# Two units of q, k, v made as one Strassen-like group of seven products, in a planned kernel for windowed attention beside an MLP

## The chip, the cores and the metric

The kernel runs on one core of one Trainium2 chip. The metric is device microseconds of that core for one execution; the time before is the median of three executions. A profile is one further execution, recorded instruction by instruction.

## The reference, cut to what matters

The input x has 2048 positions (S) of 640 numbers (D). Everything is float32. Two branches read it, and a gate mixes them:

```python
x = A_x
g = sigmoid((x * gate_w).sum(-1, keepdims=True))
# branch A: 32 heads of 20, window of 8 keys at distance 0, 2, 4 ... 14
qkv = x @ A_wqkv                       # (2048, 640) @ (640, 1920)
logits[s, w] = q[s] . k[s - 2 * w] * 20 ** -0.5
o[s] = sum_w softmax(logits)[s, w] * v[s - 2 * w]
a = o @ A_wo                           # (2048, 640) @ (640, 640)
# branch B: Dense, Mish, Dense
h = x @ B_w1 + B_b1                    # (2048, 640) @ (640, 1728)
b = (h * tanh(softplus(h))) @ B_w2     # (2048, 1728) @ (1728, 640)
return g * a + (1 - g) * b
```

## The kernel before, in words

**Products.** TensorE (PE) multiplies blocks of 128x128 by 128 rows of up to 512 columns. To keep float32 accuracy each operand is held as a pair of tiles, a rounded part (`hi`) and what is left of it (`lo`), and one product is three matmuls: hi·hi, hi·lo, lo·hi (`mm3`, lines 462 to 464). Making a pair is called a split: ScalarE (ACT) copies the raw tile to `hi` (line 412), and VectorE (DVE) or GpSimd (POOL) subtracts to get `lo` (line 415).

**The work is cut so.** The 2048 positions are two halves P = 0 and 1, each of two blocks of 512 (`tb`). Eight units u make q, k and v: unit u is half P = u // 4 and eight heads `hq` = u % 4; its weights are 496 columns wide (480 of q, k, v and 16 of the first dense layer; 512 for hq = 0, which carries the gate too). A unit has eight slots of 128 positions; a slot is 5 blocks of D times 3 matmuls, 15 matmuls, summed in one PSUM bank of the ring `qb` and then copied out by three ACT instructions (`qkv_evac`, lines 626 to 630) to the tile `kvq`. The first dense layer (`Quad` for P = 0, `Plain` for P = 1) makes two blocks of 128 hidden values for a whole half. In a `Quad` a 2x2 product of blocks is done with seven products, as in Strassen's method: weight and x blocks are added and subtracted beforehand (`combined`, line 816; `x_forms`), some banks are seeded from others by ACT (`seed`, line 920), and DVE adds two banks at the end (`added`, line 936). The forms of x for that, `FORM[P, "t1" .. "t4", i]`, lie in SBUF. `sums_of` prepares added blocks of w2 and wo in the same way. Then come the second dense layer (`mlp2`) and the output projection (`wo_part`), for P = 0 and P = 1.

**Attention** runs on DVE, unit by unit, beside the PE's work: for each pair of slots a multiply q·k (line 519), a reduction over the 20 numbers of a head (522), a softmax of four slots (maximum 540, subtraction 541, exp on ACT 542, a copy of the weights on ACT 543, sum 548, reciprocal 549, times the gate 550, weights times that 551), multiplies with v (560) and a reduction over the window (564). The result is turned (line 475) and written to DRAM as `o`.

**What sets the order.** The kernel's text adds tasks to a planner (`Plan`); each has an engine, a cost in ns, tasks that it waits for and buffers that it takes from rings (three PSUM banks each in `qb` and `sb`, 24 pairs, 8 raw tiles, 6 tiles `hb`). `Plan.run` plays these costs through and gives each engine a fixed list of instructions; on the chip every engine follows its list and waits on semaphores. When several tasks are ready, the one with the lowest rank goes first, then the one that was added first. So the order in which the text calls `unit`, `quads`, `mlp1_last` and so on sets the order on PE, and DVE takes attention steps only where no task of lower rank is ready. Tasks for `"ANY"` go to POOL, or to DVE where they are due (`NEAR`, `PATIENCE`). Transfers are issued by SyncE (SP), line 429; the planner takes `LAG["SP"]` ns and the size for their landing.

**Lines that the prediction speaks of.** 412 and 415 (split), 462 to 464 (matmuls), 519, 522, 560, 564 (the four long attention steps), 475 (turn), 816 (sum of two tiles), 920 (seed), 926 (Mish of the first layer), 936 (sum of two banks), 626 to 630 (a slot's way out of PSUM), 1173 (sums behind the second dense layer's products).

Of the kernel before, what the change touches and what calls it, by code (L numbers as in the profile page):

```python
# [30 lines left out]
ROW = 2 * QF  # L31
# [35 lines left out]
class Plan:  # L67


    NEAR, PATIENCE = 8000, 2000  # L70
# [34 lines left out]
    def run(self):  # L105
# [34 lines left out]

        def fits(t):
            want = {}
            for b in t.take:
                want[b.ring] = want.get(b.ring, 0) + 1
                if b.ring.free < want[b.ring] or b.ring.line[b.ring.at + want[b.ring] - 1] is not b:
                    return False
            return True

        while left:
            again = not events or events[0][0] > now  # L150
            while again:
                again = False
                for e in self.LAG:
# [41 lines left out]
                    if e == "PE":  # L195
                        begun_pe = max(begun_pe, t.pos)
                    busy[e] = again = True
# [6 lines left out]
                    if e != "SP":  # L204
# [12 lines left out]
            if what == "done":  # L217
                left -= 1
                x.at = now
                for b in x.hold:  # L220
# [5 lines left out]
            for t in x.then:  # L226

                if (t.eng == x.eng and x.eng != "SP") != (what == "own"):
# [7 lines left out]
        return now  # L236


@with_exitstack
def kernel(ctx: ExitStack, tc: tile.TileContext, x, wq, wo, w1, b1, w2, out):  # L240
# [12 lines left out]
    NPAIR, NRAW, NH = 24, 8, 6  # L253
# [110 lines left out]
    w1_d = {(q, n): dram.tile([128, 2, 512], F32, name=f"wf{q}_{n}") for q in range(NQUAD + 1) for n in range(4)}  # L364
    h_d = [dram.tile([FR, 512], F32, name=f"h{tb}") for tb in range(4)]
# [133 lines left out]
    def attention(u, P, hq, ready, gates):  # L499
# [29 lines left out]
        def bounded(a, b, after):  # L529
# [4 lines left out]
            return add("ACT", 130 * (min(b, 7) - a), run, cg + after, rank=-1)  # L534

        def softmax(a, rank, after, used):
# [4 lines left out]
            t = step("DVE", 350, lambda: V.tensor_tensor(lg[:, h], lg[:, h], mx[:, h, :, None].to_broadcast([128, 4, HQ, W]), op=OP.subtract))  # L541
            e = add("ACT", 360 + 2 * TABLE, lambda: A.activation(lg[:, h], lg[:, h], AF.Exp, scale=scale), [t], rank=-1, late=1500)
            return e, add("ACT", 600, lambda: A.activation(pw_h[:, h], lg[:, h], AF.Copy), [e, used], rank=-1)

        def shares(a, rank, e, copied):
# [4 lines left out]
            step("DVE", 230, lambda: V.tensor_tensor(sm[:, h], sm[:, h], gate[:, P, h, None].to_broadcast([128, 4, HQ]), op=OP.mult), gates)  # L550
# [85 lines left out]
    def qkv(u, P, hq, between={}):  # L636
        n = columns(u)
        kv = KV[UNIT[u]]
        ev = {}
        pss = [sb_buf() if i == 3 else qb_buf() for i in range(4 if u == 0 else 0)]  # L640
        if u == 0:
# [14 lines left out]
            for kc in range(2, KC):  # L656
                for i in range(4):
# [3 lines left out]
                    if kc == KC - 1:  # L661
                        ev[i] = qkv_evac(u, P, hq, i, pss[i], last)
        for i in range(8):
            if i in ev:
                continue
            if len(pss) == i:
                pss.append(qb_buf())

            def slot(i=i):
                for kc in range(KC):  # L670
                    qkv_part(pss[i], P, u, i, kc, n)

            xs = [X[2 * P + i // 4, kc] for kc in range(KC)]
            ws = [WQ[u, kc] for kc in range(KC)]
            last = pe_add(15 * mm_ns(n), slot, sum((b.ready for b in xs + ws), []), take=[pss[i]], hold=xs + ws)
            ev[i] = qkv_evac(u, P, hq, i, pss[i], last)
            if i in between:
                between[i]()
        before = sum((freed.get((BEFORE.get(u), s), []) for s in range(8)), [])
        halo = {}  # L680
        for lo, hi, src in ((3, 7, (0, 1, 2, 3)), (0, 3, (5, 6, 7))):
            w = [ev[i][0] for i in src] + before + cg
            halo[lo] = [dma(lambda a=a, b=b, lo=lo, hi=hi: kv[a + 1:b + 1, lo:hi], lambda a=a, b=b, lo=lo, hi=hi: kv[a:b, lo + 8:hi + 8],
                            w, rank=-1.0, size=(b - a) * (hi - lo) * ROW * 4) for a, b in ((0, 112), (112, 127))]
# [1022 lines left out]
```

## Time and profile before

| | |
|---|---|
| three executions | 623.71, 624.12, 624.54 us; median 624.12 us |
| the profiled execution | 624.5 us, of which 622.7 us lie between its first and last instruction |
| busy share of that span | PE 99%, weight loads 82%, DVE 93%, ACT 56%, POOL 48% |
| matmuls | 2743 in the trace |
| bytes moved | 140.36 MB, mean 225 GB/s |
| granted TensorE clock | 1.000 |

The span is what the profile's times count in; the 1.8 us between it and the execution's own time lie before the first and after the last instruction. A matmul's time in the rows is modelled and longer than its share of the engine, since matmuls are pipelined: the distance from one start to the next is what it costs. Waits are listed by who ended them. "Busy" on PE therefore says only that there was no gap.

### The profile page before, as it was taken

The page shows a single profiled execution, that of the slowest core. Times are in us where ns is not written, and L with a number is a line of the kernel's source. Part 1 is how long each engine was busy: PE and PEld are TensorE (multiplying, and loading weights), DVE is VectorE, ACT ScalarE, POOL GpSimd, SP SyncE. Part 2 cuts the span into 40 slices and gives each one's busy share as a digit, 9 for nine tenths or more (in the row PEclk, how much of TensorE's full clock was granted, in tenths as well). Part 3 has the DMA queues.
Part 4 walks back from the last instruction along what each step waited for, and adds up shares of the span by engine and source line. Part 5 has one row for each costly group of instructions (what it writes and reads, how often), then busy time and mean ns, then how long its engine had stood idle before and what let it go on. Part 6 is the DMA issues. An engine that isn't in the chain of part 4 may idle for free.

```text
span 622.7 us, 9060 instructions
## 1 busy us (share of the span) xinstructions
PE 616.9 (99%) x2743; PEld 513.3 (82%) x2743; DVE 578.8 (93%) x554; ACT 351.3 (56%) x790; POOL 299.6 (48%) x277
## 2 busy tenths in 40 slices
PE   9999999999999999999999999999999999999997
PEld 7878888888888888888888888888888888888886
DVE  7799999999999999999999999999999999869965
ACT  6687637746675554634664545676655634546520
POOL 1487657575576557567553614787318610100000
PEclk9999999999999999999999999999999999999999
DMA  8765675595784779989976687768798755999613
GB/s 309 210 191 156 241 254 130 180 294 155 253 279 147 250 236 252 270 253 274 281 229 212 210 281 191 206 177 247 225 323 260 196 189 179 246 291 337 229 53 118
DMA packets 97600, 140.36 MB, mean 225 GB/s; under 512 B 11200, under 2 KB 51392, under 8 KB 97328
## 3 DMA queue, kind: packets, MB, share of 16 engines
q1 hardware_dynamic: 94192, 134.02, 67.3%
q0 software_dynamic: 3072, 5.51, 5.8%
q8 instruction: 21, 0.34, 0.3%
q10 hardware_dynamic: 288, 0.26, 0.1%
q14 instruction: 27, 0.22, 0.1%
HBM read 87.78 MB, written 51.00 MB: 223 GB/s over the span
## 4 chain that ended last, share of the span: by engine, by line
PE 96%; ACT 1%; DVE 1%; issue 0%; POOL 0%; DVEq 0%
PE qb L462 20%; PE qb L463 20%; PE qb L464 20%; PE sb L462 11%; PE sb L463 11%; PE sb L464 11%; PE qb L620 1%; ACT pair L412 1%; DVE raw L816 1%; PE sb L394 1%; DVE pair L415 0%; PE qb L468 0%; PE sb L469 0%; PE sb L468 0%; PE qb L469 0%
## 5 line engine op out<-in xcount | busy, mean ns | idle before, releaser
L415 POOL TENSOR_TENSOR pair<-raw,pair 128x512 fp32r<-128x512 f32 (+3 forms) x131 | 162.5, 1269 | 100.0 <-ACT pair L412 51.2
L462 PE MATMUL qb<-pair 128*128 128x512 f32 (+1 forms) x467 | 180.7, 387 | 1.0 <-ACT hb L740 1.0
L463 PE MATMUL qb<-pair 128*128 128x512 f32 (+1 forms) x467 | 180.6, 387 | 0.0
L464 PE MATMUL qb<-pair 128*128 128x512 f32 (+1 forms) x467 | 180.6, 387 | 0.0
L412 ACT ACTIVATE pair<-raw 128x512 fp32r<-128x512 f32 (+3 forms) x223 | 128.6, 610 | 56.3 <-DMA raw<-actt 18.0
L463 PE MATMUL sb<-pair 128*128 128x512 f32 (+1 forms) x294 | 113.7, 387 | 0.0
L464 PE MATMUL sb<-pair 128*128 128x512 f32 (+1 forms) x294 | 113.7, 387 | 0.0
L462 PE MATMUL sb<-pair 128*128 128x512 f32 (+1 forms) x294 | 113.7, 387 | 0.0
L462 PEld LDWEIGHTS qb<-pair 128*128 128x128 f32 x467 | 87.7, 188 | 18.5 <-ACT hb L740 1.4
L464 PEld LDWEIGHTS qb<-pair 128*128 128x128 f32 x467 | 87.6, 188 | 17.1
L463 PEld LDWEIGHTS qb<-pair 128*128 128x128 f32 x467 | 87.7, 188 | 17.0
L560 DVE TENSOR_TENSOR pr<-kvq,pg 128x1280 f32<-128x1280 f32 x64 | 93.1, 1484 | 1.0
L519 DVE TENSOR_TENSOR pr<-kvq,qg 128x2560 f32<-128x2560 f32 x32 | 90.0, 2811 | 2.3 <-ACT qg L525 1.0
L564 DVE TENSOR_REDUCE kvq<-pr 128x320 f32<-128x2560 f32 x32 | 90.2, 2818 | 0.9
L522 DVE TENSOR_REDUCE lg<-pr 128x128 f32<-128x2560 f32 x32 | 90.1, 2817 | 0.8
L626 ACT ACTIVATE kvq<-qb 128x320 f32<-128x320 f32 x63 | 27.6, 438 | 77.4 <-PE qb L464 77.3
L415 DVE TENSOR_TENSOR pair<-raw,pair 128x512 fp32r<-128x512 f32 (+2 forms) x92 | 64.7, 727 | 5.1 <-ACT pair L412 5.0
L464 PEld LDWEIGHTS sb<-pair 128*128 128x128 f32 x294 | 55.2, 188 | 11.3
L462 PEld LDWEIGHTS sb<-pair 128*128 128x128 f32 x294 | 55.2, 188 | 11.2
L463 PEld LDWEIGHTS sb<-pair 128*128 128x128 f32 x294 | 55.2, 188 | 11.2
L816 POOL TENSOR_TENSOR hb<-hb 128x512 f32<-128x512 f32 x38 | 50.2, 1337 | 23.8 <-DVE ot L475 5.8
L412 ACT ACTIVATE pair<-hb 128x512 fp32r<-128x512 f32 (+3 forms) x62 | 36.6, 590 | 8.7 <-PE qb L464 3.0
(158 smaller groups left out, 732.6 us busy)
## 6 DMA issues: line engine op xcount, KB each, us to landing
actt<-hb SPq DMA_DIRECT2D x52, 256.0 KB, 3.6
raw<-in_w SPq DMA_DIRECT2D x40, 256.0 KB, 4.5
act<-hb SPq DMA_DIRECT2D x38, 256.0 KB, 2.6
raw<-actt SPq DMA_DIRECT2D x37, 256.0 KB, 4.7
raw<-in_wq SPq DMA_DIRECT2D x30, 248.0 KB, 3.8
raw<-act SPq DMA_DIRECT2D x29, 256.0 KB, 2.9
raw<-in_x SPq DMA_DIRECT2D x23, 256.0 KB, 3.0
o<-ot SPq DMA_DIRECT2D x64, 80.0 KB, 2.7
```

The source lines that it names most:

```text
L394: nc.tensor.matmul(warm_banks[i % 3].t[:, :n], ones[:, :128], ones[:, :n], start=True, stop=True)
L412: a = add("ACT", act_ns(n), lambda: A.activation(hi(), raw(), AF.Copy), after, rank=rank, take=take, hold=hold)
L415: return (V if e == "DVE" else G).tensor_tensor(lo(), raw(), hi().bitcast(F32), op=OP.subtract)
L462: nc.tensor.matmul(ps, ah, bh, start=first, stop=False, skip_group_check=more)
L463: nc.tensor.matmul(ps, ah, bl, start=False, stop=False, skip_group_check=more)
L464: nc.tensor.matmul(ps, al, bh, start=False, stop=last, skip_group_check=more)
L519: return V.tensor_tensor(pr, window(kv, s0, 0), qg[:, :, None, :].to_broadcast([128, 2, W, QF]), op=OP.mult)
L522: V.tensor_reduce(lg_w[:, s0:s0 + 2], pr.rearrange("p s w (h d) -> p s w h d", d=DH), op=OP.add, axis=AX.X)
L560: V.tensor_tensor(pairs[:, s].rearrange("p k i (h d) -> p k i h d", d=DH), vw, pg[:, s0 + s].rearrange("p (k i) h -> p k i h", i=2)[:, :, ...
L564: V.tensor_reduce(q[:, s0:s0 + 2], pairs.rearrange("p s k i f -> p s f k i"), op=OP.add, axis=AX.XY)
L626: a = add("ACT", 330, lambda: A.activation(kv[:, 7 + s], ps.t[:, QF:3 * QF].rearrange("p (a b) -> p a b", a=2), AF.Copy), [done] + before, ...
L816: return (V if e == "DVE" else G).tensor_tensor(t.t[:, i:i + n], a.t[:, j:j + n], b.t[:, k:k + n], op=op)
```

## The change: what it does

Units 2 and 3 (heads 16 to 23 and 24 to 31 of the first half of x) are made together. They share x, so for four of the five blocks of D (0 to 3, taken as the pairs 0 with 2 and 1 with 3) the weights of the two units and the two 512-position blocks of x form 2x2 products of blocks, and these are done with seven products in place of eight, with the forms of x that the quads already have. Block 4 stays as it was (`plain`). The new class `Two` holds this, for each j of four 128-position slots:

- first stage: `a1` (s1·t1, 6 matmuls, copied by ACT to an `hb` tile and stored to DRAM), `a2` (11·x, 6 matmuls, then a DVE sum to a bank of `sb`), `a3` (s2·t2, 6 matmuls into that sum, copied by ACT and stored), `b1` and `b2` (9 matmuls each), which end two slots of unit 2;
- second stage: `c0` loads the two stored tiles, `c1` seeds a bank of `sb` from one of them by ACT, adds s3·t3 (6 matmuls), and DVE subtracts the other to a bank of `qb`; `c2` (3 matmuls) and `c3` (9 matmuls) end two slots of unit 3.

Weights are loaded as raw tiles in two goes (`wa`, `wc`), combined (eight combinations of 128x496) and split (16 pairs in place of 10). The planner counts how many transfers are in flight on SP and starts no more than eight 450-ns issues' worth; `LAG["SP"]` is 2700 for 3000, `ADDING` 4000 for 6000, `PATIENCE` 1000 for 2000; a task that sends data itself is followed when it has landed. The gate now goes into the copy of the softmax weights: four ACT instructions of 128x64 with a scale in place of one of 128x256, and DVE's multiply by the gate (line 550) is gone. The order of the steps is a list of names, `ORDER`, in place of calls with `between`; the parts of a quad (`first`, `second`, `m1` to `m4`, `l1`, `l2`) and the slots of a unit can stand there one by one. All second-half quads stay `Plain` (`KIND`), so the classes for another kind are not used.

```diff
-    NEAR, PATIENCE = 8000, 2000
+    NEAR, PATIENCE = 8000, 1000
-    LAG = {"PE": 220, "ACT": 220, "DVE": 200, "POOL": 150, "SP": 3000}
+    LAG = {"PE": 220, "ACT": 220, "DVE": 200, "POOL": 150, "SP": 2700}
-    ADDING = 6000
+    ADDING = 4000
+    FLIGHT = 8
...
+        def lanes(t):
+            return round(t.ns / 450)
...
-                    fit = [t for t in ready[e] if fits(t)]
+                    fit = [t for t in ready[e] if fits(t) and (e != "SP" or flight + lanes(t) <= self.FLIGHT)]
...
+KIND = 'PPPPPP'
+PAIRS = {2: (0, 1)}
+ORDER = """
+u.0.5 u.0.7 u.0.4 last.0 u.0.6 q.0.0.first pieces.0.1 q.0.0.m1 q.0.1.first wq.1 pieces.0.2 q.0.1.second q.0.0.second q.0.0.m3 q.0.0.m4 q.0.1.m1 last.1
...
+pieces.0.5 q.0.5.first q.0.4.l1 p.2.3.c0 q.0.5.m1 q.0.5.m4 q.0.5.second x.3.3 q.0.5.m2 x.2.1 x.3.0 p.2.0.c1 p.2.1.c1 x.3.4 p.2.0.c2 q.0.5.m3 p.2.3.c1
...
-            return e, add("ACT", 600, lambda: A.activation(pw_h[:, h], lg[:, h], AF.Copy), [e, used], rank=-1)
+            def weighted():
+                for i in range(a, a + 4):
+                    A.activation(pw_h[:, i], lg[:, i], AF.Copy, scale=gate[:, P, i:i + 1])
+
+            return e, add("ACT", 1200, weighted, [e, used] + gates, rank=-1)
...
-            step("DVE", 230, lambda: V.tensor_tensor(sm[:, h], sm[:, h], gate[:, P, h, None].to_broadcast([128, 4, HQ]), op=OP.mult), gates)
...
+        def copy(self, to, of, n, after, take=()):
+            return add("ACT", act_ns(n) + 60, lambda: A.activation(to.t[:, :n], of.t[:, :n], AF.Copy), after, rank=-0.5, take=take, hold=[to, of])
+
+        def sum_to(self, to, x, y, op, n, after, yt=None):
+            yt = yt or (lambda: y.t)
+            return add("DVE", dve_ns(n) + 80, lambda: V.tensor_tensor(to.t[:, :n], x.t[:, :n], yt()[:, :n], op=op), after, rank=SOON, kind="psum",
+                       take=[to], hold=[to, x, y])
...
+        def a1(self, j):
+            n, ep, v = self.n, qb_buf(), h_buf()
+            t = self.products(ep, j, self.fs("s1", "t1"), [], n, [ep], True)
+            self.copied[j] = c = self.copy(v, ep, n, [t], [v])
...
+            self.state["v", j] = self.store(v_d[self.u, j], v, NCOL, [c])
+
+        def a2(self, j):
+            n, al, be = self.n, qb_buf(), sb_buf()
+            t = self.products(al, j, self.xs("11", 0, 0), [], n, [al], True)
+            self.al[j], self.be[j] = al, be
+            self.seeded[j] = self.sum_to(be, al, self.v[j], OP.add, n, [t, self.copied[j]])
...
+        def b1(self, j):
+            t = self.products(self.al[j], j, self.xs("12", 0, 1) + self.plain(0, 0), [self.seeded[j]], self.n)
+            units[self.u].ready(j, self.al[j], t)
...
+        def c1(self, j):
+            ga, de, n = sb_buf(), qb_buf(), NCOL
+            (u, ut, du), (v, vt, dv) = self.state["u", j], self.state["v", j]
+            s = add("ACT", act_ns(n) + 60, lambda: A.activation(ga.t[:, :n], ut()[:, :n], AF.Copy), [du], rank=-0.5, take=[ga], hold=[ga, u])
+            t = self.products(ga, j, self.fs("s3", "t3"), [s], n)
+            self.ga[j], self.de[j] = ga, de
+            self.seeded[j] = self.sum_to(de, ga, v, OP.subtract, n, [t, dv], vt)
+
+        def c2(self, j):
+            t = self.products(self.ga[j], j, self.plain(1, 1), [self.seeded[j]], NCOL)
+            units[self.u + 1].ready(4 + j, self.ga[j], t)
+
+        def c3(self, j):
+            t = self.products(self.de[j], j, self.fs("22", "t4") + self.plain(1, 0), [self.seeded[j]], NCOL)
+            units[self.u + 1].ready(j, self.de[j], t)
```

Where the instructions stand now, at the end of the first half, just before unit 4 begins. On PE there stood the last four slots of unit 3, of 15 matmuls each, all from bank to bank of `qb` with no other engine between them; the first matmul of each, and of unit 4 behind them:

```order
L462 MATMUL qb_2026<-pair_1691,kvq2_262 128x496
...
L462 MATMUL qb_2057<-pair_1691,kvq2_262 128x496
...
L462 MATMUL qb_2086<-pair_1691,kvq2_262 128x496
...
L462 MATMUL qb_2118<-pair_1691,kvq2_262 128x496
...
L462 MATMUL qb_2143<-pair_2017,pair_1843 128x512
```

Now the last product of the quads (into sb_1972) stands there and behind it the second stage of the pair, again the first matmul of each group. `c1` of three slots j are the groups into sb_2029, sb_2034, sb_2046, each of 6 matmuls; the second group into sb_2029 is its `c2`, qb_2072 its `c3`:

```order
L494 MATMUL sb_1972<-pair_576,pair_1796 128x512
...
L494 MATMUL sb_2029<-pair_1655,pair_573 128x496
...
L494 MATMUL sb_2034<-pair_1655,pair_573 128x496
...
L494 MATMUL sb_2046<-pair_1655,pair_573 128x496
...
L494 MATMUL sb_2029<-pair_1729,pair_431 128x496
...
L494 MATMUL qb_2072<-pair_1690,pair_576 128x496
...
L494 MATMUL sb_2046<-pair_1729,pair_431 128x496
...
L494 MATMUL qb_2080<-pair_1690,pair_576 128x496
...
L494 MATMUL sb_2121<-pair_1655,pair_573 128x496
```

Groups of 15 that waited for no other engine's result became groups of 3 to 9 of which each waits for an ACT copy or a DVE sum.

On DVE, at the same place, there were attention steps (kvq0 and kvq1 are the q, k, v of two units, pr the products) and splits of weights and x for unit 4:

```order
L564 TENSOR_REDUCE kvq0_260<-pr_267 128x320
L519 TENSOR_TENSOR pr_267<-kvq0_260,qg_266 128x2560
L522 TENSOR_REDUCE lg_263<-pr_267 128x2x8x8
L560 TENSOR_TENSOR pr_267<-kvq0_260,pg_265 128x4x2x160
L415 TENSOR_TENSOR pair_2055<-raw_2007,pair_2055 128x512
L415 TENSOR_TENSOR pair_2082<-raw_2045,pair_2082 128x512
L540 TENSOR_REDUCE mx_268<-lg_263 128x32
L541 TENSOR_TENSOR lg_263<-lg_263,mx_268 128x256
```

Now the sums of the second stage (line 808, PSUM to PSUM) stand among them, the first of them behind an attention reduction (line 554, which was 522):

```order
L1144 TENSOR_TENSOR hb_2017<-hb_2009,sb_1890 128x512
L1144 TENSOR_TENSOR hb_2009<-hb_2009,sb_1932 128x512
L447 TENSOR_TENSOR pair_2020<-raw_1959,pair_2020 128x512
L572 TENSOR_REDUCE mx_276<-lg_271 128x32
L573 TENSOR_TENSOR lg_271<-lg_271,mx_276 128x256
L554 TENSOR_REDUCE lg_271<-pr_275 128x2x8x8
L808 TENSOR_TENSOR qb_2072<-sb_2029,pair_1741 128x496
L808 TENSOR_TENSOR qb_2075<-sb_2034,pair_1759 128x496
L808 TENSOR_TENSOR qb_2080<-sb_2046,pair_1861 128x496
L551 TENSOR_TENSOR pr_275<-kvq0_268,qg_274 128x2560
L554 TENSOR_REDUCE lg_271<-pr_275 128x2x8x8
L808 TENSOR_TENSOR qb_2155<-sb_2121,pair_1938 128x496
```

The bank that sb_2029 takes is free once an `added` sum (the two rows of line 1144, which was 936) has read it; the `c2` and `c3` groups on PE wait for the rows of line 808.

On ACT there were a split, the last slots' way out of PSUM and the softmax's bounds:

```order
L412 ACTIVATE pair_2082<-raw_2045 128x512
L626 ACTIVATE kvq1_261<-qb_2057 128x320
L628 ACTIVATE kvq1_261<-qb_2057 128x160
L532 ACTIVATE lg_263<-bound_76 1x8x7
L532 ACTIVATE lg_263<-bound_76 1x8x6
```

Now the seeds of the second stage (line 861) stand behind the Mish of the quads' last product (line 1132, which was 926):

```order
L444 ACTIVATE pair_2020<-raw_1959 128x512
L1132 ACTIVATE hb_2025<-sb_1972,bias_75 128x512
L861 ACTIVATE sb_2029<-pair_1741 128x496
L861 ACTIVATE sb_2034<-pair_1759 128x496
L861 ACTIVATE sb_2046<-pair_1861 128x496
L1132 ACTIVATE hb_2017<-hb_2017,bias_75 128x512
L1132 ACTIVATE hb_2009<-hb_2009,bias_75 128x512
L574 ACT_TABLE_LOAD
```

So the first `c1` on PE follows the PE group just before it only by way of two ACT instructions.

More of the change, by code (lines that the diff above doesn't have):

```diff
@@ L661, in qkv @@
                     if kc == KC - 1:
[L662 to L684, printed above, removed]
-        own = sum((list(ev[i][:2]) for i in range(8)), [])
@@ L686, in qkv, with ready @@
[L686 to L690 removed]
+                        self.ev[i] = qkv_evac(u, P, self.hq, i, pss[i], last)
+        def ready(self, i, ps, t):
+            self.ev[i] = qkv_evac(self.u, self.P, self.hq, i, ps, t)
+            quads_done.append(self.ev[i][2])
+            if len(self.ev) == 8:
+                self.ended()
@@ new lines, in slot, with run @@
+        def slot(self, i):
+            u, P, n = self.u, self.P, self.n
+            if i not in self.ev:
+                ps = qb_buf()
+                def run():
+                    for kc in range(KC):
+                        qkv_part(ps, P, u, i, kc, n)
+                xs = [X[2 * P + i // 4, kc] for kc in range(KC)]
+                ws = [WQ[u, kc] for kc in range(KC)]
+                t = pe_add(15 * mm_ns(n), run, sum((b.ready for b in xs + ws), []), take=[ps], hold=xs + ws)
+                self.ev[i] = qkv_evac(u, P, self.hq, i, ps, t)
+            if len(self.ev) == 8:
+                self.ended()
```

348 lines of the change are left out of this document (250 added, 98 removed).

## The prediction

> **What bounds the kernel now.** I read the page first: the share of each engine and the slices.
>
> ```profile
> span 622.7 us, 9060 instructions
> PE 616.9 (99%) x2743; PEld 513.3 (82%) x2743; DVE 578.8 (93%) x554; ACT 351.3 (56%) x790; POOL 299.6 (48%) x277
> ```
>
> PE has no room and DVE little. Next the waits of PE, which are two in the whole execution, together 1.8 us:
>
> ```profile
> PE qb L462 <- ACT hb L740: 1.0, 1, 1.0
> PE sb L394 <- PEq L1695: 0.8, 1, 0.8
> ```
>
> Then the stretches of 50 us. The columns are PE, weight loads, DVE, ACT, POOL, each with its count, then the granted clock, the DMA share and GB/s:
>
> ```profile
> 100.00:150.00 50.00, 50.00 (x226) 42.07 (x225) 48.00 (x38) 30.71 (x73) 31.74 (x31) 1.00 0.64 198
> 150.00:200.00 50.00, 50.00 (x226) 42.07 (x225) 47.61 (x41) 33.06 (x78) 33.13 (x28) 1.00 0.69 218
> ...
> 250.00:300.00 50.00, 50.00 (x225) 41.99 (x224) 49.00 (x36) 24.97 (x64) 30.33 (x31) 1.00 0.92 269
> ```
>
> PE is full in each and the clock stays at 1.00, so the time is matmuls times their spacing. DVE is the next engine: 48 to 49 of 50 us in the first half. A matmul taken away shortens the program only if DVE, which must then do its list in less time, doesn't make PE wait.
>
> **The matmuls removed.** For each of four j the group ends four slots (two of each unit) with 54 matmuls in place of 4 x 15 = 60, so 216 stand for 240: 24 matmuls of 496 columns go. Their price is the distance from start to start; between these two rows lie 24 starts:
>
> ```profile
> 129.94 0.38 PE L462 MATMUL qb<-pair 128*128 128x496 f32 x1
> 135.22 0.38 PE L462 MATMUL qb<-pair 128*128 128x496 f32 x1
> ```
>
> 5.28 us for 24, 0.220 each. The same count with 512 columns, used below, gives 0.2267:
>
> ```profile
> 429.64 0.39 PE L462 MATMUL sb<-pair 128*128 128x512 f32 x1
> 435.08 0.39 PE L462 MATMUL qb<-pair 128*128 128x512 f32 x1
> ```
>
> So the change takes 5.28 us from PE's work.
>
> The Trainium skill ("TensorE: Matmul & The Clock Gate", section "Wait — 56ns, not 53.3ns?") puts a streaming matmul at one column per cycle of 2.4 GHz and about 2.5 ns more. By that, an estimate, 496 columns are 209 ns and the 24 matmuls 5.0 us; the rows show 5% more per matmul, and the rows decide.
>
> **The waits added on PE.** They lie at the end of the first half, where c1, c2 and c3 stand. First the way through ACT. The seed of c1's bank stands on ACT behind the Mish of the PE group just ahead. The rows for each step: the last matmul of a slot and the start of the copy that it releases, then the Mish and a seed (mean ns of one):
>
> ```profile
> 138.96 0.38 PE L464 MATMUL qb<-pair 128*128 128x496 f32 x1
> 139.38 0.44 ACT L626 ACTIVATE kvq<-qb 128x320 f32<-128x320 f32 x1 [1.86 <-PE qb L464]
> L926 ACT ACTIVATE hb<-sb,bias 128x512 f32<-128x512 f32 x18 | 12.3, 683 | 14.4 <-PE sb L464 9.4 <-DMA actt<-hb 4.3 <-ACT hb L926 0.7
> L920 ACT ACTIVATE sb<-sb 128x512 f32<-128x512 f32 x12 | 7.1, 588 | 3.9 <-PE sb L464 3.7
> ```
>
> 0.42 from start to ACT, 0.68, 0.59, less the 0.23 that the matmul itself takes: PE waits 1.5 us at least.
>
> Second, the way through DVE. c2 and c3 wait for the first sum of line 808, row 139 of DVE's new list, behind all the attention steps that stand there before it. So I count both engines from the end of unit 0, which is where DVE's attention can start, to that sum. DVE's prices:
>
> ```profile
> L560 DVE TENSOR_TENSOR pr<-kvq,pg 128x1280 f32<-128x1280 f32 x64 | 93.1, 1484 | 1.0
> L564 DVE TENSOR_REDUCE kvq<-pr 128x320 f32<-128x2560 f32 x32 | 90.2, 2818 | 0.9
> L522 DVE TENSOR_REDUCE lg<-pr 128x128 f32<-128x2560 f32 x32 | 90.1, 2817 | 0.8
> L519 DVE TENSOR_TENSOR pr<-kvq,qg 128x2560 f32<-128x2560 f32 x32 | 90.0, 2811 | 2.3 <-ACT qg L525 1.0
> L415 DVE TENSOR_TENSOR pair<-raw,pair 128x512 fp32r<-128x512 f32 x83 | 59.6, 738 | 5.1 <-ACT pair L412 5.0
> L475 DVE STREAM_TRANSPOSE ot<-kvq 128x640 f32<-128x640 f32 x16 | 13.5, 842 | 0.3
> L936 DVE TENSOR_TENSOR hb<-hb,sb 128x512 f32<-128x512 f32 x12 | 8.1, 677 | 1.1 <-PE sb L464 0.8
> L541 DVE TENSOR_TENSOR lg<-lg,mx 128x256 f32<-128x256 f32 x16 | 7.0, 440 | 0.6
> L550 DVE TENSOR_TENSOR sm<-sm,gate 128x32 f32<-128x32 f32 x16 | 4.1, 259 | 0.4
> ```
>
> In DVE's new list, from the first q·k to the first sum of line 808 stand 11 multiplies and 11 reductions of q·k (61.9 us), 16 multiplies with v (23.7), 8 reductions over the window (22.5), 23 sums of two tiles of whatever line (at 0.68, 15.6), 6 splits (4.4), 4 turns (3.4) and 26 short softmax and gate steps (10.7, most of them like the row of line 541): 142.2 us. The means count too much, since neighbours overlap. Before, the stretch between the first row and the last one here holds 130.7 us by means and took 131.5, of which 3.0 were waits (1.1 for a transfer, the rest short ones for ACT and PE); so means give 128.5/130.7 = 0.983 of themselves, 139.8 us:
>
> ```profile
> 36.13 2.81 DVE L519 TENSOR_TENSOR pr<-kvq,qg 128x2560 f32<-128x2560 f32 x1
> ...
> 102.68 0.68 DVE L936 TENSOR_TENSOR hb<-hb,sb 128x512 f32<-128x512 f32 x1
> 103.28 2.81 DVE L522 TENSOR_REDUCE lg<-pr 128x128 f32<-128x2560 f32 x1
> ...
> 167.66 2.81 DVE L519 TENSOR_TENSOR pr<-kvq,qg 128x2560 f32<-128x2560 f32 x1
> ```
>
> PE has in the same stretch 339 matmuls of 512 columns (76.9 us) and 282 of 496 (62.0): 138.9 us. DVE starts some 1.6 us after the end of unit 0 (the copies out of PSUM and the spreading of q, by rows like the one at 139.38). So PE waits 139.8 + 1.6 − 138.9 = 2.5 us if DVE never waits, and 5.5 if its 3.0 us of waits come back. A count from the last place where DVE must wait for PE (the sum into hb_1707, 27 DVE rows ahead: 37.8 us by means, less the 0.08 that each of 18 short steps overlaps, as from 102.68 to 103.28; PE 34.6 us; 0.3 for the handing over) gives 2.0, the lower end. I take half of the DVE waits: 4.0 us. The wait of 1.0 at 42 us lies in this stretch too and is in that figure, so it comes off once: gain 5.28 + 1.0 − 4.0 = 2.3 us.
>
> **What costs nothing, with its cover.** SP gets 22 more transfers of about 0.25 MB, 5.5 MB on 140.4; they fall mostly between 70 and 170 us, where the DMA share is 0.64 to 0.69, and at 0.92 (250 to 300 us) PE didn't wait either. If that cover fails, c1's reload comes late at one transfer's wait, about the 1.1 us above. POOL's eight combinations and some splits are 10 us more on 48%. ACT gets 12 copies (7 us), and 64 weight copies of 128x64 for 16 of 128x256. No row has 128x64; the nearest are narrower and wider:
>
> ```profile
> L543 ACT ACTIVATE pw<-lg 128x256 f32<-128x256 f32 x16 | 11.4, 713 | 0.5
> L630 ACT ACTIVATE hx<-qb 128x16 f32<-128x16 f32 x63 | 11.9, 189 | 0.0
> L1025 ACT ACTIVATE raw<-raw 128x128 f32<-128x128 f32 x9 | 2.7, 314 | 0.0
> ```
>
> Four take 0.76 to 1.26 us for 0.71; I take 1.0, +4.6 us in all. DVE's sum and reciprocal hide it, and if they don't, DVE waits 0.3 us sixteen times, mostly where it has waits anyway. The multiply of line 550 frees DVE 16 × 0.259 = 4.1 us, the eight sums cost it 8 × 0.68 = 5.4. The planner's numbers move only the order.
>
> **The sum.** 624.5 of the profiled execution less 2.3 is 622.2. The median lies 0.4 under that execution: 621.8.
>
> **Rivals.** *PE waits only for the short way* (2.0 us or, if ACT alone decides, 1.5): 5.28 + 1.0 − 2.0 = 4.3 off, 619.8; 619.3 to 620.8. For it: before, DVE's list held PE up nowhere. Against: DVE's list is counted longer than PE's.
>
> *The waits fill the gain*: more of the c groups, each 3 to 9 matmuls, wait in turn, 5.1 to 7.5 us in all: 622.9 to 625.3.
>
> *DVE is late in the second half* (slower than before). The attention of units 4 to 7 moves back in DVE's list: its last reduction over the window stood at 507.7 us and is counted about 13 us later. Before, DVE waits there:
>
> ```profile
> 506.00 0.69 DVE L1173 TENSOR_TENSOR kvq<-kvq,sb 128x512 f32<-128x512 f32 x1 [0.43 <-PE sb L469]
> 507.14 0.69 DVE L1173 TENSOR_TENSOR kvq<-kvq,sb 128x512 f32<-128x512 f32 x1 [0.45 <-PE sb L469]
> 507.74 2.81 DVE L564 TENSOR_REDUCE kvq<-pr 128x320 f32<-128x2560 f32 x1
> ...
> 531.79 0.69 DVE L1173 TENSOR_TENSOR kvq<-kvq,hb 128x512 f32<-128x512 f32 x1 [3.98 <-ACT hb L1169]
> ...
> 552.70 0.69 DVE L1173 TENSOR_TENSOR kvq<-kvq,qb 128x512 f32<-128x512 f32 x1 [5.37 <-PE qb L469]
> ```
>
> 10.2 us of room, so PE was never held. Now, from the c groups to the projection's late splits, PE has 1147 and 411 matmuls (350.4 us) and DVE's 260 instructions come to 346 by means: 4.4 us of room. If DVE meets such waits again before that point, it is 10.2 − 4.4 = 5.8 late and PE waits for its splits: 621.8 + 5.8 = 627.6 (625.4 to 629). It is slower than before once those waits pass 4.4 + 2.3 + 1.2 = 7.9 us. For it: the two long waits show that DVE's list is not dense there. Against: a later attention leaves DVE work where it waited.
>
> *The clock falls.* Each wait on PE in this trace was 1.0 us or less, and the clock stayed at 1.00. At the start matmuls lie further apart:
>
> ```profile
> 0.80 3.15 PE sb L394 x10
> ...
> 5.33 0.85 PE qb L620 x2
> 6.18 0.25 PE sb L620
> 6.43 0.70 PE qb L620 x3
> ```
>
> 0.425 us each at 5.33, 0.233 each from 6.43 on: 5.4 us from 0.80 at about half pace. If a wait of 4 us in one piece brought that back, half of it, 2.7 us, would be lost: 624.5, up to 626. Against: the wait is likely in two pieces.
>
> The Trainium skill (same page, section "What's actually happening") says that an idle window of about 3.4 us makes the clock fall to half. Before has no such gap, so no row here bears it out.
>
> That the matmuls do not go is no case: PE's new list has them fewer.
>
> **How the numbers follow.** Forecast 0.42 (620.8 to 622.8), short way 0.09, waits fill the gain 0.20, DVE late 0.22, clock 0.07. A measurement here tells about 0.2%, 1.25 us, from no change: 622.9 and 625.3 are the bounds. Faster is 0.42 + 0.09 = 0.51; within is 0.20, and 0.02 of the clock's; slower 0.22 + 0.05 = 0.27. The range leaves out the upper part of the DVE case and the lowest of the short way: 619.5 to 627.6. The cases of the forecast's sign alone give 619.3 to 622.8.
>
> **What would show it.** Right: 2719 to 2721 matmuls; PE waits of 2 to 5.5 us in all between 168 and 182 us (unit 0's end near 36, then the 138.9 us of matmuls), the larger for a sum of line 808, the other for a seed of line 861; none over 1 us behind it; the clock at 1.00. Wrong: PE waits for splits after 450 us (DVE late), waits for transfers at the c groups, a clock below 1.00 there, or sums of line 808 that are done before PE comes (short way).

## The result, and the profile after

The changed kernel takes 621.9 us (median of 7 executions, 620.57 to 622.46) beside 623.88 us of the kernel before: ratio 0.9962, 95% interval 0.9951 to 0.9974. The forecast was 621.8. As the sections below show, the sum came out for a partly different reason than the prediction gave. Two executions lie far above all others of their kernel (3041.09 us of one of the kernel before, 686.61 us of one with a longer DVE, at a clock of 0.849) and are in no median or ratio.

The page of the profiled execution (622.0 us), the lines of share and count:

```profile
span 620.2 us, 9150 instructions
PE 613.0 (99%) x2719; PEld 509.3 (82%) x2719; DVE 583.5 (94%) x550; ACT 364.4 (59%) x854; POOL 312.6 (50%) x287
```

24 matmuls are gone (2743 to 2719), and DVE is busier by 4.7 us in a span shorter by 2.5. All the waits of PE:

```profile
PE sb L494 <- ACT sb L861: 1.8, 1, 1.8
PE sb L426 <- PEq L1933: 0.8, 1, 0.8
PE qb L656 <- DVE kvq L1729: 0.7, 1, 0.7
```

The wait of 1.0 us at 42 us is gone, and the seed of the first `c1` (line 861) costs 1.8 us. The wait of 0.7 at the start is new but costs nothing: the first group of three matmuls behind it begins at 6.39 us, at 6.43 in the kernel before. No wait for a sum of line 808 stands here. What does stand here is a loss that the list of waits cannot show. The stretches around the c groups, with PE's busy time and count, then the granted clock, the DMA share and GB/s:

```profile
168.00:172.00 4.00, 3.36 (x15) 1.00 0.98 325
172.00:174.00 2.00, 0.87 (x4) 1.00 0.94 306
174.00:176.00 2.00, 2.00 (x7) 0.56 1.04 375
176.00:178.00 2.00, 2.00 (x7) 0.59 1.04 382
178.00:180.00 2.00, 2.00 (x11) 1.00 1.05 364
```

PE is "busy" all through 174 to 178, but only 7 matmuls run in each 2 us, in whole or in part, beside 11 from 178 to 180: the granted clock is 0.56 and 0.59. If the clock was at half while it was down, that is (0.44 + 0.41) x 2 / 0.5 = 3.4 us at half. The same place matmul by matmul:

```profile
170.97 0.39 PE L496 MATMUL sb<-kvq,pair 128*128 128x512 f32 x1
173.13 0.49 PE L494 MATMUL sb<-pair 128*128 128x496 f32 x1 [1.77 <-ACT sb L861]
...
174.45 0.61 PE L496 MATMUL sb<-pair 128*128 128x496 f32 x1
...
176.93 0.61 PE L496 MATMUL sb<-pair 128*128 128x496 f32 x1
177.34 0.54 PE L494 MATMUL sb<-pair 128*128 128x496 f32 x1
...
177.93 0.39 PE L496 MATMUL sb<-pair 128*128 128x496 f32 x1
```

From 171.20 (the last matmul's start and its 0.23) to 173.13 PE has nothing for 1.93 us. From 174.45 to 176.93 six steps take 2.48 us, 0.413 each in place of 0.220. The nine long steps from 174.13 to 177.72 add up to 1.6 us over 0.22 each.

This does not happen in every execution. Of the 12 of the changed kernel measured here and in a later run, six had a mean clock of 1.000 and took 620.57 to 621.51 us (median 621.06), six had 0.996 or 0.997 and took 621.66 to 622.46 (median 621.97). The 621.9 is the median of seven of which four had the fall. The repeated run's profile is of an execution without it, and there PE does lose a little to a sum of line 808, too short for the list of waits: the last matmul of the third `c1` and the first of `c2` lie 0.41 us apart in place of 0.22, and the first sum on DVE has just ended:

```profile
177.47 0.39 PE L496 MATMUL sb<-pair 128*128 128x496 f32 x1
177.88 0.50 PE L494 MATMUL sb<-pair 128*128 128x496 f32 x1
```

```profile
177.16 1.83 DVE L808 TENSOR_TENSOR qb<-sb,pair 128x496 f32<-128x496 f32 x3
```

### The profile page after: what moved, and what is told of

It reads as the page before. It is cut to its first block, busy times and chain, and to the rows that moved or that the text cites. A ratio compares the mean times of both kernels' runs of the same rounds, so it can differ in the third digit from the quotient of the medians.

```text
span 620.2 us, 9150 instructions
## 1 busy us (share of the span) xinstructions
PE 613.0 (99%) x2719; PEld 509.3 (82%) x2719; DVE 583.5 (94%) x550; ACT 364.4 (59%) x854; POOL 312.6 (50%) x287
## 4 chain that ended last, share of the span: by engine, by line
PE 98%; DMA 0%; DVE 0%; ACT 0%; issue 0%; SPq 0%; DVEq 0%
PE qb L494 20%; PE qb L495 20%; PE qb L496 20%; PE sb L494 12%; PE sb L495 12%; PE sb L496 12%; PE qb L656 1%; DMA raw<-in_wq 0%; PE qb L500 0%; PE sb L501 0%; PE sb L500 0%; PE qb L501 0%; PE sb L656 0%; DVE pair L1722 0%; ACT hb L1132 0%
## 5 line engine op out<-in xcount | busy, mean ns | idle before, releaser
L447 POOL TENSOR_TENSOR pair<-raw,pair 128x512 fp32r<-128x512 f32 (+4 forms) x127 | 156.3, 1250 | 105.0 <-ACT pair L444 63.3
L496 PE MATMUL qb<-pair 128*128 128x512 f32 (+1 forms) x451 | 174.5, 387 | 0.0
L494 PE MATMUL qb<-pair 128*128 128x512 f32 (+1 forms) x451 | 174.5, 387 | 0.0
L495 PE MATMUL qb<-pair 128*128 128x512 f32 (+1 forms) x451 | 174.5, 387 | 0.0
L444 ACT ACTIVATE pair<-raw 128x512 fp32r<-128x512 f32 (+2 forms) x229 | 133.5, 608 | 62.7 <-DMA raw<-actt 19.7
L494 PE MATMUL sb<-pair 128*128 128x512 f32 (+2 forms) x326 | 126.8, 389 | 1.8 <-ACT sb L861 1.8
L496 PE MATMUL sb<-pair 128*128 128x512 f32 (+2 forms) x326 | 126.7, 389 | 0.0
L495 PE MATMUL sb<-pair 128*128 128x512 f32 (+2 forms) x326 | 126.6, 388 | 0.0
L494 PEld LDWEIGHTS qb<-pair 128*128 128x128 f32 x451 | 84.7, 188 | 16.7
L496 PEld LDWEIGHTS qb<-pair 128*128 128x128 f32 x451 | 84.7, 188 | 16.6
L495 PEld LDWEIGHTS qb<-pair 128*128 128x128 f32 x451 | 84.7, 188 | 16.5
L447 DVE TENSOR_TENSOR pair<-raw,pair 128x512 fp32r<-128x512 f32 (+2 forms) x102 | 71.4, 720 | 4.6 <-ACT pair L444 4.5
L494 PEld LDWEIGHTS sb<-pair 128*128 128x128 f32 x326 | 61.7, 189 | 14.6 <-ACT sb L861 2.2
L496 PEld LDWEIGHTS sb<-pair 128*128 128x128 f32 x326 | 61.5, 189 | 12.5
L495 PEld LDWEIGHTS sb<-pair 128*128 128x128 f32 x326 | 61.6, 189 | 12.3
L662 ACT ACTIVATE kvq<-qb 128x320 f32<-128x320 f32 x55 | 24.0, 437 | 57.2 <-PE qb L496 57.1
L999 POOL TENSOR_TENSOR hb<-hb 128x512 f32<-128x512 f32 x34 | 44.2, 1307 | 24.5 <-ACT hb L1132 11.3
L999 POOL TENSOR_TENSOR raw<-raw 128x256 f32<-128x256 f32 (+2 forms) x31 | 31.2, 1013 | 15.2 <-DVE pg L587 3.6
```

The source lines that it names most:

```text
L444: a = add("ACT", act_ns(n), lambda: A.activation(hi(), raw(), AF.Copy), after, rank=rank, take=take, hold=hold)
L447: return (V if e == "DVE" else G).tensor_tensor(lo(), raw(), hi().bitcast(F32), op=OP.subtract)
L494: nc.tensor.matmul(ps, ah, bh, start=first, stop=False, skip_group_check=more)
L495: nc.tensor.matmul(ps, ah, bl, start=False, stop=False, skip_group_check=more)
L496: nc.tensor.matmul(ps, al, bh, start=False, stop=last, skip_group_check=more)
L662: a = add("ACT", 330, lambda: A.activation(kv[:, 7 + s], ps.t[:, QF:3 * QF].rearrange("p (a b) -> p a b", a=2), AF.Copy), [done] + before, ...
```

## The experiments

There were two theories at first. Theory 1: the seed's wait, and the fall of the clock behind it, are what keep the change from its 5.3 us. Theory 2, as predicted: DVE's list holds PE at the c groups, and the clock plays no part. All medians below are of one launch on one core; ratios are to the kernel before, measured beside each.

**Matmuls that only keep PE at work.** The tile `qg` got the rest of its PSUM bank, and 20 products of a constant go there ahead of the first `c1`:

```diff
+                for _ in range(fill):
+                    nc.tensor.matmul(idle, ones[:, :128], ones[:, :128], start=True, stop=True)
                 for k, (w, x) in enumerate(todo):
```

> The changed kernel with 20 small matmuls (128 columns of a constant, into an unused part of the bank of qg) put on PE just ahead of the first c1, so that they run while its seed is awaited; nothing is left out. Theory 1 (the wait of 1.8 us for the seed pulls TensorE's clock to about half for 8 matmuls in part of the executions, 1.3 us of the median): the clock is 1.000 in every execution and the time is that of the changed kernel's undisturbed executions, 620.6 to 621.2 us, beside 621.9 of its median. Theory 2 (what was predicted: DVE's list holds PE back, the clock plays no part): nothing changes, 621.9.

Measured: 621.09 us (620.4 to 621.11), ratio 0.9946 (0.9934 to 0.9958), clock 0.999 or 1.000 in all five. PE's rows:

```profile
171.45 0.39 PE L499 MATMUL sb<-kvq,pair 128*128 128x512 f32 x1
171.68 1.34 PE L791 MATMUL qg<-const-bfloat16-1.0 128*128 128x128 bf16 x20
173.61 0.49 PE L497 MATMUL sb<-pair 128*128 128x496 f32 x1 [0.59 <-ACT sb L866]
```

The seed is no earlier (PE goes on 1.93 us after the last product would have ended, as before), but the matmuls behind it keep their 0.22 us. Repeated beside the changed kernel itself on one chip, with 8 in place of 20 as a third:

> The changed kernel itself, beside the two fillings on the same chip. Both theories: 621.9 us as median; theory 1 adds that its executions fall into two groups, 620.5 to 621.5 at a clock of 1.000 and 621.9 to 622.5 at 0.997.

> The changed kernel with the 20 small matmuls ahead of the first c1 once more, for a comparison on one chip. Theory 1 (the fall of the clock is what they prevent): 620.4 to 621.1 us, the clock at 0.999 or 1.000 in every execution, 0.8 us less than the changed kernel's median. Theory 2 (the clock plays no part): the same as the changed kernel.

> The same with 8 small matmuls in place of 20: of PE's 1.9 us without work some 1.4 are left, between the 1.2 at 41 us of the kernel before (clock at 0.998 in 8 of 39 executions) and the 1.9 of the changed kernel (0.997 in 4 of 7). Theory 1, if the chance of a fall grows with the length of the gap: a fall in 1 or 2 of 5 executions, median 620.6 to 621.3. Theory 2: the same as the changed kernel, 621.9.

Measured: the changed kernel 621.17 us (three executions at 1.000: 620.96 to 621.17; two at 0.996 and 0.997: 621.66 and 622.45), 20 matmuls 621.34 (620.67 to 622.0), 8 matmuls 620.76 (620.35 to 621.64). None of the 15 filled executions had a clock below 0.999, against six of twelve of the changed kernel. On the one chip alone it is none of ten against two of five, which would show little; taken together, and with the next run, it says that the filling prevents the fall. What that is worth in time is smaller than I expected: the ratios to the kernel before are 0.996 (0.9947 to 0.9972), 0.9956 (0.9944 to 0.9969) and 0.9953 (0.994 to 0.9967), whose intervals overlap. In the profile of the second filling another wait had come up at 84 us (0.6 us for line 669); the repeated changed kernel loses 0.25 us at the same place, so it is not the filling's. A version that surely beats the changed kernel was not found.

**A longer wait.** The first seed copied three times:

```diff
-            s = add("ACT", act_ns(n) + 60, lambda: A.activation(ga.t[:, :n], ut()[:, :n], AF.Copy), [du], rank=-0.5, take=[ga], hold=[ga, u])
+            s = add("ACT", act_ns(n) + 60, lambda: [A.activation(ga.t[:, :n], ut()[:, :n], AF.Copy) for _ in range(1 if j else 3)], [du], rank=-0.5, take=[ga], hold=[ga, u])
```

> The changed kernel with the first c1's seed copied three times in place of once, 1.1 us more on ACT before PE goes on. Theory 1: PE's wait grows from 1.8 to 2.9 us and the clock falls in every execution: 620.7 + 1.1 + 1.6 = 623.4 us, a few tenths less where DVE's sum was awaited anyway. Theory 2 (DVE's list sets when c2 starts): PE waits for the seed in place of the sum, 621.9 to 622.3.

Measured: 623.11 us (ratio 0.9984, 0.9973 to 0.9994). The wait is 3.0 us, and nine of twelve executions show 0.996 or 0.997 (median 623.5), not every one, as theory 1 had it; the other three took 621.3 to 622.8. In the profiled one the slow steps begin with the first matmul and end near 177.7, as in the changed kernel:

```profile
174.25 0.78 PE L494 MATMUL sb<-pair 128*128 128x496 f32 x1 [3.01 <-ACT sb L861]
174.83 0.61 PE L495 MATMUL sb<-pair 128*128 128x496 f32 x1
175.24 0.61 PE L496 MATMUL sb<-pair 128*128 128x496 f32 x1
...
177.31 0.54 PE L495 MATMUL sb<-pair 128*128 128x496 f32 x1
177.68 0.39 PE L496 MATMUL sb<-pair 128*128 128x496 f32 x1
```

Theory 2's 621.9 to 622.3 is out where the clock falls: the wait is 1.2 us longer and the nine executions 1.5 us slower than the changed kernel's six with a fall. So the seed is on the path.

**A longer DVE.** The reduction ahead of the first sum done twice:

```diff
-                V.tensor_reduce(lg_w[:, s0:s0 + 2], pr.rearrange("p s w (h d) -> p s w h d", d=DH), op=OP.add, axis=AX.X)
+                nth.append(0)
+                for _ in range(2 if len(nth) == 11 else 1):
+                    V.tensor_reduce(lg_w[:, s0:s0 + 2], pr.rearrange("p s w (h d) -> p s w h d", d=DH), op=OP.add, axis=AX.X)
```

> The changed kernel with the attention reduction just ahead of the first sum of line 808 done twice: 2.8 us more on DVE before the sums. Theory 1 (in the trace the first sum ends 1.5 us before PE comes to c2, or about as PE comes where the clock didn't fall): PE waits 1.4 us (with the fall) to 2.9 us (without) more, 623.4 us; a wait of nearly 3 us may bring a second fall of the clock, up to 625. Theory 2 (DVE is what holds PE): the whole 2.8 us, 624.7.

Measured: 625.04 us as median of eleven executions, ratio 1.0013 (1.0005 to 1.0022); nine of them are at 0.997 or less, the two at 1.000 took 623.3 and 624.0. One profile, at a clock of 1.000, answers more than the time. PE's waits of this kernel:

```profile
PE sb L494 <- DVE qb L811: 2.7, 1, 2.7
PE sb L494 <- ACT sb L864: 1.8, 1, 1.8
```

and DVE's rows:

```profile
173.74 5.67 DVE L557 TENSOR_REDUCE lg<-pr 128x128 f32<-128x2560 f32 x2
179.32 1.84 DVE L811 TENSOR_TENSOR qb<-sb,pair 128x496 f32<-128x496 f32 x3
```

Of 2.8 us added, 2.7 became a wait. So without the fall DVE has next to no room: PE and DVE come to `c2` together, as the repeated run's rows above show. Theory 2 was not wrong about DVE; the seed's wait just fills the same time. Where the clock falls, PE is later and DVE has more room.

**The gate on DVE again.** One copy of the weights on ACT, and a multiply behind each reciprocal; the order stays:

```diff
-                for i in range(a, a + 4):
-                    A.activation(pw_h[:, i], lg[:, i], AF.Copy, scale=gate[:, P, i:i + 1])
+                A.activation(pw_h[:, h], lg[:, h], AF.Copy)
...
+                V.reciprocal(sm[:, h], sm[:, h])
+                return V.tensor_tensor(sm[:, h], sm[:, h], gate[:, P, h, None].to_broadcast([128, 4, HQ]), op=OP.mult)
```

> The changed kernel with the gate multiplied on DVE again (one instruction more behind each of 16 reciprocals, 0.26 us each) and one ACT copy of the softmax weights in place of four. Nothing else moves. Four of the 16 lie before the c groups: DVE's first sum comes 1.0 us later. Theory 1 (DVE's sum and PE come to c2 nearly together where the clock doesn't fall, and DVE is 1.6 us early where it does): 0 to 1.0 us more, 621.9 to 622.6 as median. Theory 2 (DVE is what holds PE, and holds it later as well): 1.0 us or more, 622.9 and above. Rival: ACT's shorter copies let DVE start its shares earlier, and nothing changes or it gets faster: 621.5.

Measured: 621.81 us (620.64 to 622.79), ratio 0.996 (0.9947 to 0.9972): no difference that this can tell. Its profile now has the tie on the other side:

```profile
PE sb L494 <- ACT sb L866: 1.8, 1, 1.8
...
PE sb L494 <- DVE qb L813: 0.3, 1, 0.3
```

The 1.0 us did not reach the sum, since DVE had waits to lose. Two of the repeated changed kernel's trace, 1.2 us in all,

```profile
97.48 0.69 DVE L1144 TENSOR_TENSOR hb<-hb,sb 128x512 f32<-128x512 f32 x1 [0.72 <-PE sb L496]
141.39 0.69 DVE L1144 TENSOR_TENSOR hb<-hb,sb 128x512 f32<-128x512 f32 x1 [0.47 <-DMA kvq<-kvq]
```

are gone here, with one of 0.64 us at 172.09 in their place, and the first sum begins 0.4 us later (177.59 in place of 177.16). The run says one thing more: its gap on PE is the same 1.93 us, and none of its five executions has a clock below 0.998.

**The 24 matmuls alone.** The kernel before, without one of five blocks of D in unit 3 (that part of q, k, v is left out):

```diff
                 for kc in range(KC):
-                    qkv_part(pss[i], P, u, i, kc, n)
+                    if (u, kc) != (3, 2):
+                        qkv_part(pss[i], P, u, i, kc, n)
```

> The kernel before with one of the five blocks of D left out of unit 3 (3 matmuls of 496 columns in each of its 8 slots, 24 in all); all else stays. Theory 1 (the matmuls cost their spacing, and DVE would have followed a faster PE): 5.28 us less, 618.7 us beside 624.0. Theory 2 (DVE's list is what stands behind PE, with under 4 us of room): PE gets waits of 1 to 5 us, 619.7 to 623.

Measured: 622.81 us, ratio 0.9976 (0.9963 to 0.9989): 1.5 us less, not 5.3. PE's waits are now

```profile
PE qb L462 <- ACT hx L630: 2.0, 1, 2.0
PE qb L462 <- ACT hb L741: 1.0, 1, 1.0
PE sb L394 <- PEq L1696: 0.8, 1, 0.8
PE qb L462 <- ACT hb L927: 0.8, 1, 0.8
```

The wait of 2.0 us is DVE's. At the beginning of unit 4 ACT stands before it with nothing to do, and behind a turn:

```profile
195.41 0.74 ACT L578 ACTIVATE ot<-ot 128x640 f32<-128x640 f32 x1 [2.57 <-DVE ot L475]
196.05 0.29 ACT L628 ACTIVATE kvq<-qb 128x160 f32<-128x160 f32 x1
```

The slot's way out of PSUM (line 628 and 630) waits on ACT behind that copy of the turned tile, and PE waits for the bank. In the profile this gives 5.28 - 2.0 - 0.8 = 2.5, and 624.5 to 622.4 is 2.1; two more of its six executions show a clock of 0.997. The wait of 0.8 us lies at 358 us, where the Mish (line 927) stands on ACT behind a softmax, a copy that waited 0.27 us for DVE, and a table load of 1.28 us. Theory 1's 618.7 is out, and theory 2's DVE is real in the kernel before also: its list has room for less than half of the 24 matmuls.

**The pair undone.** The changed kernel with units 2 and 3 as plain slots at the places where the pair ended them:

```diff
...
-p.2.2.c0 p.2.2.c1 q.0.5.l1 p.2.3.c2 x.2.2 p.2.3.c3 x.3.2 x.2.3 p.2.2.c3 p.2.2.c2 x.3.1 p.2.0.c3 p.2.1.c3 p.2.1.c2 x.2.4 q.0.5.l2 wq.4 x.2.0 third sum
...
+q.0.5.l1 u.3.7 x.2.2 u.3.3 x.3.2 x.2.3 u.3.2 u.3.6 x.3.1 u.3.0 u.3.1 u.3.5 x.2.4 q.0.5.l2 wq.4 x.2.0 third sum
```

> The changed kernel with units 2 and 3 made plainly again: each step of the list that ended a slot of the pair (b1, b2, c2, c3) is that slot of 15 matmuls, the steps a1 to a3, c0, c1 are gone, and the weights are loaded as before. The planner's numbers, the list of steps and the softmax weights stay as changed. Theory 1 (the gain is the 24 matmuls less the wait and the fall of the clock at the c groups; the rest of the change gives only the 0.3 us at the start): 5.3 us more matmuls, 1.8 us less wait, the clock at 1.000: 620.7 + 5.3 - 1.8 = 624.2 us, within 0.4 of the kernel before. Theory 3 (the gain is from the new order and the planner's numbers): 621.9 or less.

Measured: 625.49 us, ratio 1.002 (1.0011 to 1.0029). Theory 3 is out, and theory 1's 624.2 is 1.3 too low. PE's waits are 0.8, 0.7 and 0.5 us. By the two ratios the pair is worth (1.002 - 0.9962) x 624 = 3.6 us; against the changed kernel's executions without the fall it is 625.49 - 621.06 = 4.4 (5.28 less 1.3 of waits would be 4.0). The rest of the change (list, planner's numbers, softmax weights) costs 0.002 x 624 = 1.2 us in this kernel, which I had put at a gain of 0.3. Where that lies stays open: PE's waits add up to only 0.2 us more than before.

**Two tries at a better order**, both misses. In the first, nine independent matmuls were held back to cover the seed:

```diff
-            t = self.mms(self.al, self.two(0, 256, self.x(0, 1)) + self.k4(0, 0), [self.sb])
+            t = self.mms(self.al, self.two(0, 256, self.x(0, 1)) + self.k4(0, 0), [self.sb] + ([self.l2t] if self.cover else []))
```

> The changed kernel with nine independent matmuls of the last quad (its m2) moved between the quads' last product and the first c1 on PE, and its second product put where m2 stood: PE has 2.0 us of work while the first seed is made. Theory 1: the wait for the seed (1.8 us) and the fall of the clock go; PE then comes to c2 about 1.9 us before DVE's first sum is done (it stands behind a reduction of 2.8 us), so a wait for line 808 of 1.5 to 2 us takes its place, which may pull the clock down as well: 620.7 to 622. Theory 2 (DVE alone holds PE): the same wait, no clock: 621.9.

Measured: 627.75 us, ratio 1.0058 (1.0046 to 1.007). PE still waits 2.1 us for the seed, since the Mish ahead of it on ACT now waits for a hidden tile that a store still holds:

```profile
172.22 0.69 ACT L1133 ACTIVATE hb<-sb,bias 128x512 f32<-128x512 f32 x1 [1.73 <-DMA actt<-hb]
```

and at 193 us unit 4 waits 3.2 us for a split, with the clock at 0.50 from 194 to 196. In the second, the first `c1` takes its bank from `qb`, and two sums go ahead of the reduction (further lines, not shown, hold PE's order there):

```diff
-            ga, de, n = sb_buf(), qb_buf(), NCOL
+            ga, de, n = (qb_buf(), sb_buf(), NCOL) if j in SWAP else (sb_buf(), qb_buf(), NCOL)
...
+            if j in FIRST:
+                self.seeded[j].then.append(reds[10])
+                reds[10].waits += 1
+                before(self.seeded[j], sums5[4])
```

> The changed kernel with two edits at the c groups: the first c1 takes its bank from qb in place of sb (it is free early, so its seed doesn't wait for the Mish of the quads' last product), and the first two sums of line 808 stand on DVE ahead of the attention reduction of 2.8 us that they stood behind. Nothing is left out; PE's order there stays that of the changed kernel but for one group. Theory 1 (these two waits, and the clock that falls behind the first, are what keeps the change from its 5.3 us): PE waits under 1 us at the c groups, the clock is 1.000, and the time is 620.6 - 1.8 + 0.5 = 619.3 us, 619 to 620. Rival (as in the run with the moved product): a store that holds a hidden tile or a late split for unit 4 takes the wait's place: 621 us and above.

Measured: 635.73 us, ratio 1.018 (1.0166 to 1.0194). On ACT the softmax, with a table load on either side, had come to stand ahead of the seeds:

```profile
169.26 1.28 ACT L578 ACT_TABLE_LOAD   x1
...
174.55 1.28 ACT L1150 ACT_TABLE_LOAD   x1
...
177.61 1.09 ACT L870 ACTIVATE sb<-pair 128x496 f32<-128x496 f32 x2
```

PE waited 5.7 us for them, and 4.7 us in all for splits after 400 us; the clock was at 0.50 from 176 to 182 us and again from 454 to 458. Both kernels were planned anew from an edit of one place, and the plan moved others.

## Why the prediction was right, and where it was wrong

**The matmuls: right.** 24 fewer, at 0.220 us each. The rest by distances from start to start: the kernel before lost 1.18 us at the wait at 42 us and 0.11 in the step behind it; after, 1.93 and 0.11 are lost at the seed, 1.6 in slow steps and 0.11 at 68 us. 5.28 + 1.29 - 2.04 - 1.6 - 0.1 = 2.8, against 2.5 between the profiled executions; the other 0.3 is spread over steps that are each longer by less than 0.06 us.

**The way through ACT: the path right, one instruction left out.** At least 1.5 us was the floor; counted in the same way it is 1.93. A split stands between PE's last matmul (170.97) and the Mish, which the count passed over:

```profile
171.40 0.63 ACT L444 ACTIVATE pair<-raw 128x512 fp32r<-128x512 f32 x1 [0.25 <-PE sb L496]
171.93 0.67 ACT L1132 ACTIVATE hb<-sb,bias 128x512 f32<-128x512 f32 x1
172.50 1.59 ACT L861 ACTIVATE sb<-pair 128x496 f32<-128x496 f32 x3
```

**The way through DVE: the mechanism right, its size too large.** Taken was 4.0 us in all, between 2.5 (DVE never waits) and 5.5. From the first q·k to the end of the first sum:

```profile
37.29 2.82 DVE L551 TENSOR_TENSOR pr<-kvq,qg 128x2560 f32<-128x2560 f32 x1 [0.46 <-ACT qg L557]
...
176.59 0.67 DVE L808 TENSOR_TENSOR qb<-sb,pair 128x496 f32<-128x496 f32 x1
```

That is 140.0 us, of which 0.5 are waits; the count by means gave 139.8 without waits. In the repeated run, without the fall, it is 140.5 with 1.2 of waits. In that run PE loses 2.04 us to the seed (1.93, and 0.11 in the step behind it) and 0.19 to the sum: 2.2 in place of 4.0. What failed is the size of a difference of two sums near 140 us, of which four terms were each a little off, all in one direction. "I take half of the DVE waits" put 1.5 us where there are 1.2 (0.5 in the profiled execution); DVE starts 1.2 us behind unit 0's end, not 1.6; its work without waits is 139.3 us, not 139.8; and PE takes 0.6 us more than the 138.9 to come there (0.11 at 68 us and 0.36 at 84 in gaps, the rest spread). Without anything else the time is that of the six executions without a fall, median 621.06, between the rival *short way* (619.3 to 620.8) and the forecast.

**The clock: given 0.07, and it happened in half of the executions.** It was tied to a wait of 4 us in one piece. A gap of 1.93 us did it, at 1.6 us for the matmuls, of which 0.9 remains between the medians. A PE that comes later no longer meets DVE, which gives back 0.3 (0.19 at the sum and 0.12 in the step behind it); where the other 0.4 goes was not found. The fall filled the gap between 621.06 and the 621.8 predicted. The forecast's number therefore rests on two errors of about 1 to 1.7 us with opposite signs, and its closeness is luck. Of the signs that the prediction named for "right", the 2719 matmuls came and no wait over 1 us stands behind the c groups, but PE's wait there is 1.8 us, not 2 to 5.5, and the larger part is not for a sum of line 808. Two signs for "wrong" came, in the profiled execution: a clock below 1.00 at the c groups, and a first sum that is done (177.26) before PE comes (178.83).

The Trainium skill ("TensorE: Matmul & The Clock Gate", section "What's actually happening") gives an idle window of about 3.4 us for the fall and the same time at work for the rise. The second agrees with the 3.4 us at half clock here; for the first, the runs have the fall after 1.93 us without work in some executions and not in others, so the measurement decides.

**The rival on DVE in the second half: not so.** The attention did move back as counted. Its last reduction over the window, and the longest waits of DVE between 500 and 580 us that are left:

```profile
521.41 2.81 DVE L600 TENSOR_REDUCE kvq<-pr 128x320 f32<-128x2560 f32 x1
```

```profile
DVE kvq L1388 <- PE qb L501: 1.6, 1, 1.6
DVE kvq L1388 <- PE sb L501: 0.8, 2, 0.4
```

It stood at 507.74, so it is 13.7 us later, and the two waits of 4.0 and 5.4 us have become one of 1.6. The later attention filled them, as the "against" of that rival said.

**Covers.** The 22 transfers caused no wait on PE, and of ACT's extra copies only the first seed did. Four weight copies take 1.14 us on ACT (1.0 taken); putting the gate back on DVE changed nothing that can be measured.

## What to carry to other kernels

Before work is taken from the engine that is full, leave it out in a trial that keeps everyone's order: here 24 matmuls of 5.28 us gave 1.5, since the second engine was right behind. Count that engine's list to the meeting point from its rows, and carry over an old wait only where the new order still has its cause. On the way between two engines list every instruction: a split on ACT that was passed over cost 0.5 us of the wait. After each new gap on TensorE, read the granted clock and the distance between starts, not the busy share: the loss behind a gap of 1.93 us was 1.6 us here.

## What the runs showed of the hardware

- The longer TensorE was without work, the more executions show a mean clock of 0.997 or less: none of 15 with 0.6 or 1.3 us left of the gap, 6 of 17 at 1.9 us (6 of 12 of the changed kernel, none of 5 with the gate on DVE), 9 of 12 at 3.0 us. Length alone does not decide: the profiled execution with the longer DVE had 2.9 us without work (177.13 to 180.05) at a clock of 1.000.
- A mean clock of 0.998 needs no fall between matmuls. The profiled execution with the gate on DVE shows it, with the clock at 1.00 up to 616 us and at 0.50 from 618 on, behind the last matmul. So the 0.998 in 9 of 47 executions of the kernel before is by itself no sign of a fall at its gap of 1.2 us at 41 us.
- A fall lasts about 3.4 us, by the clock of the 2 us stretches, during which matmuls of 496 columns start 0.413 us apart in place of 0.220. After 1.93 us and after 3.0 us without work it begins near 174.2, about 3 us behind the beginning of the gap, and ends near 177.6. In the try with the two sums ahead it lasts 6.8 us, twice.
- The clock records of these traces change only in steps of 3.413 us from the first rise: in the changed kernel up at 3.57, down at 174.24 (50 steps), up at 177.65 (51); in the last try up at 4.99, down at 175.66 (50), up at 182.48 (52), down at 452.13 (131). Whether the place of a gap against these steps decides if the clock falls was not tested.
- 20 matmuls of 128 columns on a constant take 1.34 us; with them, or with 8, no execution of 15 shows the fall.
